# Loading K and V of single-query attention a whole head at a time in the middle of the run, halves elsewhere

## The chip, the cores and the metric

The kernel runs on one core of one Trainium2 chip. The metric is the device time of one execution in microseconds (us). All executions quoted here are of the fast state that runs of one kernel share. "TensorE" is PE, "VectorE" is DVE, "ScalarE" is ACT, "GpSimd" is POOL, and "SyncE" is SP; SP does nothing here but issue loads. The 16 DMA engines are the units that move the data from memory into the core. The "granted clock" is the share of its full speed that TensorE was allowed to run at. A semaphore is a counter on which one engine waits until another, or a load, has raised it.

## The reference

It is attention for a single query position: 16 heads, 8192 keys, head size 256, all bfloat16.

```python
B, H, Sq, Sk, D = 1, 16, 1, 8192, 256      # q, k, v = normal * 0.05
scale = q.shape[-1] ** -0.5
scores = jnp.einsum("bhqd,bhkd->bhqk", q, k) * scale
p = softmax(scores, axis=-1)
return jnp.einsum("bhqk,bhkd->bhqd", p, v)
```

K and V are 4.19 MB each for every head and 134.22 MB in all, and every byte is used once. The arithmetic is small; the reading is the work.

## The kernel before

Each of the 128 partitions holds 64 consecutive keys of a head ("columns" 0 to 63), which are 32 KB of consecutive memory. A head's K or V is loaded as two halves of 32 columns, so a load is 128 rows of 16 KB. There are four places for K halves and four for V halves. DVE computes 24 of the 32 score columns of a half (one multiply-and-sum instruction each), PE the other 8 by transposing them. Two heads later PE multiplies the exponentials with V, one matmul per column (line L612 in the profile of before, L617 after).

The Python below first collects the program of every engine with names of results and of what to wait for; the waits become semaphore waits. SP issues the loads in the order of `items`; a load waits until the half whose place it takes has been used (`kfree`, `ktfree`, `vfree`).

```python
HALF = 32
PE_COLS = 8
GROUP = 4
UNROLL = 2
K_SLOTS = 2 * UNROLL
V_SLOTS = 2 * UNROLL
KT_SLOTS = 4
PROD = 16
FIRST_CUT = (32,)
LAST_CUT = (8, 8, 8, 4, 4)
BEFORE_CUT = (16, 16)
LAG = 4
# ... cut ...
        Kb = [sb([P, HALF * D], dt, "Kb") for _ in range(K_SLOTS)]
        Vb = [sb([P, HALF * D], dt, "Vb") for _ in range(V_SLOTS)]
        # ... cut ...
        def cols(t, h, c0, c1):
            return t[0, h].rearrange("(p j) d -> p (j d)", p=P)[:, c0 * D : c1 * D]
        # ... cut ...
        kseq = [(h, x) for h in range(H) for x in range(2)]
        NIT = 2 * H
        items, nv = [], 0
        for n, kx in enumerate(kseq):
            items.append(("k", *kx))
            while nv <= n - LAG:
                items.append(("v", *kseq[nv]))
                nv += 1
        items += [("v", *kx) for kx in kseq[nv:]]
        n_of = {kx: n for n, kx in enumerate(kseq)}


        def cuts(kind, n):
            if kind == "k" and n == 0:
                return FIRST_CUT
            if kind == "v" and n == NIT - 1:
                return LAST_CUT
            if kind == "v" and n in (NIT - 3, NIT - 2):
                return BEFORE_CUT
            return (HALF,)
        # ... cut ...
        for kind, h, x in items:
            n = n_of[(h, x)]
            slots, sem_l, t, buf = (K_SLOTS, s_k, k, Kb) if kind == "k" else (V_SLOTS, s_v, v, Vb)
            slot = n % slots
            waits = []
            if n >= slots:
                waits = [f"{kind}free{n - slots}"] + ([f"ktfree{n - slots}"] if kind == "k" else [])
            cs = cuts(kind, n)
            at = 0
            for i, wd in enumerate(cs):
                if kind == "k":
                    s = sem_l[slot] if i == 0 else s_first[i - 1]
                else:
                    s = sem_l[slot] if i == len(cs) - 1 else s_last[i + (len(LAST_CUT) - 2 + NIT - 1 - n if n < NIT - 1 else 0)]
                used[id(s)] = used.get(id(s), 0) + 16
                plan.op(
                    "sp",
                    lambda e, b=buf[slot], t=t, h=h, c=x * HALF, at=at, wd=wd: e.dma_start(
                        b[:, at * D : (at + wd) * D], cols(t, h, c + at, c + at + wd)
                    ),
                    f"{kind}{n}.{i}",
                    waits,
                    dma=(s, used[id(s)]),
                )
                at += wd
        # ... cut ...
        # DVE, for each half n and each of its first 24 columns c (the last 8 go to PE):
                    lambda e, slot=slot, c=c, col=col, h=h, r=(ttr - 1) % PROD: e.tensor_tensor_reduce(
                        out=prod[:, r * D : (r + 1) * D],
                        in0=Kb[slot][:, c * D : (c + 1) * D],
                        in1=qbc[:, sl(h) * D : (sl(h) + 1) * D],
                        scale=1.0,
                        scalar=0.0,
                        op0=ALU.mult,
                        op1=ALU.add,
                        accum_out=S[:, col : col + 1],
                    ),
        # ... cut ...
        def pv(n, c0=0, c1=HALF):
            h, x = kseq[n]
            slot = n % V_SLOTS
            a = acc[sl(h)]
            first_free = f"fin{prev(h)}" if prev(h) is not None else None
            for c in range(c0, c1):
                col = sl(h) * J + x * HALF + c
                pe(
                    lambda e, c=c, col=col: e.matmul(
                        a[0:1, 0:D],
                        lhsT=E[:, col : col + 1],
                        rhs=Vb[slot][:, c * D : (c + 1) * D],
                        start=(x == 0 and c == 0),
                        stop=(x == 1 and c == HALF - 1),
                    ),
                    f"vfree{n}" if c == HALF - 1 else None,
                    [f"e{h}", first_free] + landed("v", n, c, c + 1),
                )
        # ... cut ...
        for h in range(H):
            if h >= 2 and h % UNROLL == 0:
                plan.mark("pe")
            if h:
                softmax(h - 1)
            k_turn(2 * h)
            if h:
                softmax2(h - 1)
            k_score(2 * h)
            if h:
                lmm(h - 1)
                if h + 1 < H:
                    q_row(h + 1)
                if h >= 2:
                    pv(2 * (h - 2))
            else:
                lmm(-1, "g-1")
                for a in range(2, H // 2, 2):
                    q_rows([a, a + 1])
            k_turn(2 * h + 1)
            k_score(2 * h + 1)
            if h >= 2:
                pv(2 * (h - 2) + 1)
                final(h - 2)
        # ... cut ...
        n = 2 * (H - 2)
        pv(n)
        softmax(H - 1)
        pv(n + 1, 0, HALF // 2)
        softmax2(H - 1)
        pv(n + 1, HALF // 2, HALF)
        # ... cut ...
        n += 2
        final(H - 2)
        # ... cut ...
        pv(n)
        pv(n + 1)
        final(H - 1)
```

## Time and profile before

| | before |
|---|---|
| time, median of the first 3 runs | 322.27 us (322.23 to 323.55) |
| span in the profile, first to last instruction | 320.8 us |
| bytes loaded | 134.22 MB |
| share of the 16 DMA engines' time in the load queue | 98.7% |
| DVE busy, PE busy | 275.7 us (86%), 221.7 us (69%) |

The DMA part of the profile page of before. The first row is the mean busy share of the 16 DMA engines in tenths, in 40 equal slices of 8 us; the second is what they moved. Then come the packets, and the load queue: packets, MB, share of 16 engines' span.

```profile
DMA  7999999999999999999999999999999999999995
GB/s 304 433 435 420 427 423 431 429 425 429 430 427 429 427 425 427 429 429 427 433 429 429 429 425 425 431 427 429 428 433 427 429 426 425 429 429 429 418 417 200
DMA packets 10126, 134.36 MB, mean 419 GB/s; under 512 B 1138, under 2 KB 1155, under 8 KB 1796
q1 hardware_dynamic: 10080, 134.22, 98.7%
```

The windows view of before. The columns are: stretch, its length, busy time of each engine with the number of instructions, granted share of the TensorE clock, DMA busy share, GB/s.

```profile
40.00:80.00 40.00, 28.75 (x286) 20.38 (x286) 38.65 (x224) 11.95 (x23) 0.00 (x0) 0.96 1.00 426
120.00:260.00 140.00, 101.35 (x1003) 70.86 (x1001) 127.96 (x739) 40.98 (x81) 0.00 (x0) 0.86 1.01 428
304.00:308.00 4.00, 4.00 (x39) 3.09 (x37) 0.28 (x1) 0.34 (x1) 0.00 (x0) 1.00 1.00 418
```

The reading: by the packet records of the trace at least 16 packets, one for each engine, were under way at every moment between 5 and 300 us. With a DMA share of 1.00 at a constant rate, a faster PE or DVE should shorten nothing there; only a change of the loads themselves can. (Run 1 below shows it for PE from the other side: PE was busy for 228.0 us instead of 221.7, and the time stayed.)

The end of the chain of waits of before, in order of time (start us, length us, what):

```profile
263.39 35.08 DMA Vb<-in_v_dram
298.52 5.33 PE acc L612 x32
304.24 0.43 SPq L326
304.72 12.42 DMA Vb<-in_v_dram
317.19 1.92 PE acc L612 x16
319.13 0.47 DVE o L627
```

This piece of the chain looks like PE setting the pace: PE frees a V place at 303.9 us, SP issues the five pieces of the last V half, and the third of them lands 12.4 us after its issue. But the whole half, 2 MB, takes only 4.9 us at 428 GB/s; for the rest of the 12.4 us the load stood in the queue behind others. An earlier issue would only have lengthened its wait in the queue.

### The profile page before, as it was taken

The page shows a single profiled execution, that of the slowest core. Times are in us where ns is not written, and L with a number is a line of the kernel's source. Part 1 is how long each engine was busy: PE and PEld are TensorE (multiplying, and loading weights), DVE is VectorE, ACT ScalarE, POOL GpSimd, SP SyncE. Part 2 cuts the span into 40 slices and gives each one's busy share as a digit, 9 for nine tenths or more (in the row PEclk, how much of TensorE's full clock was granted, in tenths as well). Part 3 has the DMA queues.
Part 4 walks back from the last instruction along what each step waited for, and adds up shares of the span by engine and source line. Part 5 has one row for each costly group of instructions (what it writes and reads, how often), then busy time and mean ns, then how long its engine had stood idle before and what let it go on. Part 6 is the DMA issues. An engine that isn't in the chain of part 4 may idle for free.

```text
span 320.8 us, 6419 instructions
## 1 busy us (share of the span) xinstructions
PE 221.7 (69%) x2166; PEld 155.1 (48%) x2166; DVE 275.7 (86%) x1587; ACT 93.6 (29%) x184; POOL 1.9 (1%) x12
## 2 busy tenths in 40 slices
PE   1745239697686858585977658686667966858897
PEld 0514126565454636463655535464444644535574
DVE  0899999999999999999988988889988889888700
ACT  3453222414233242422142242312423223232010
POOL 2000000000000000000000000000000000000000
PEclk9999999979797989989597987977897797897799
DMA  7999999999999999999999999999999999999995
GB/s 304 433 435 420 427 423 431 429 425 429 430 427 429 427 425 427 429 429 427 433 429 429 429 425 425 431 427 429 428 433 427 429 426 425 429 429 429 418 417 200
DMA packets 10126, 134.36 MB, mean 419 GB/s; under 512 B 1138, under 2 KB 1155, under 8 KB 1796
## 3 DMA queue, kind: packets, MB, share of 16 engines
q1 hardware_dynamic: 10080, 134.22, 98.7%
q8 instruction: 5, 0.08, 0.1%
q14 instruction: 5, 0.04, 0.0%
q10 hardware_dynamic: 36, 0.02, 0.0%
HBM read 134.23 MB, written 0.01 MB: 418 GB/s over the span
## 4 chain that ended last, share of the span: by engine, by line
DVE 49%; DMA 45%; PE 2%; issue 2%; SPq 0%; DVEq 0%
DVE prod L367 46%; DMA Kb<-in_k_dram 30%; DMA Vb<-in_v_dram 15%; PE acc L612 2%; DVE S L367 2%; DVE g L339 0%; SPq L326 0%; DVE recip L348 0%; DVE m L386 0%; DVEq L158 0%; DVE o L627 0%; DVEq L155 0%; DVEq L152 0%
## 5 line engine op out<-in xcount | busy, mean ns | idle before, releaser
L367 DVE CUSTOM_DVE_ANT_0 prod<-Kb,qbc 128x256 bf16<-128x256 bf16 x768 | 269.1, 411 | 27.1 <-DMA Kb<-in_k_dram 24.7
L612 PE MATMUL acc<-Vb,E 128*1 128x256 bf16 x1024 | 146.9, 313 | 7.8 <-DMA Vb<-in_v_dram 7.7
L612 PEld LDWEIGHTS acc<-Vb,E 128*1 128x1 bf16 x1024 | 95.9, 96 | 51.1 <-DMA Vb<-in_v_dram 9.0
L507 ACT ACTIVATE KT<-tp 128x1024 bf16<-128x1024 bf16 x64 | 62.0, 1021 | 116.1 <-PE tp L498 116.1
L367 DVE DVE_READ_ACCUMULATOR2_ANT S<- 128x1 f32 x768 | 56.8, 74 | 0.0
L498 PE MATMUL tp<-identb,Kb 128*128 128x128 bf16 x512 | 38.2, 234 | 5.0 <-DMA Kb<-in_k_dram 5.0
L498 PEld LDWEIGHTS tp<-identb,Kb 128*128 128x128 bf16 x512 | 32.3, 105 | 13.0 <-issue 10.6
L524 PE MATMUL spe<-qcur,KT 128*128 128x1 bf16 x512 | 20.6, 165 | 19.6 <-ACT KT L507 19.6
L563 PE MATMUL misc<-g,ones_row 1*128 1x1 f32 x32 | 7.1, 287 | 37.2 <-DVE g L339 37.2
L524 PEld LDWEIGHTS spe<-qcur,KT 128*128 128x128 bf16 x512 | 16.4, 98 | 24.5 <-ACT KT L507 24.3
L563 PEld LDWEIGHTS misc<-g,ones_row 1*128 1x128 f32 x32 | 5.7, 221 | 40.2 <-DVE g L339 40.0
L635 ACT ACTIVATE o<-acc,recip 1x256 bf16<-1x256 f32 x15 | 7.0, 466 | 60.7 <-PE acc L612 60.7
L552 PE MATMUL misc<-ident,m 128*1 128x128 f32 x34 | 7.1, 293 | 18.2 <-DVE m L386 18.2
L552 PEld LDWEIGHTS misc<-ident,m 128*1 128x1 f32 x34 | 1.8, 81 | 22.0 <-DVE m L386 21.6
L570 ACT ACTIVATE negb<-misc 128x1 f32<-128x1 f32 x16 | 2.7, 171 | 27.6 <-PE misc L563 27.6
L339 DVE TENSOR_REDUCE g<-misc 1x1 f32<-1x128 f32 x17 | 4.7, 274 | 5.2 <-PE misc L552 5.2
L627 DVE TENSOR_SCALAR o<-acc,recip 1x256 bf16<-1x256 f32 x1 | 0.5, 471 | 7.5 <-PE acc L612 7.5
L592 PE MATMUL misc<-ones_col,lsum 128*1 128x1 f32 x34 | 3.2, 164 | 4.1 <-ACT E L577 3.7
L577 ACT ACTIVATE E<-S,negb 128x64 bf16<-128x64 f32 x16 | 5.6, 349 | 0.7 <-ACT negb L570 0.2
L348 DVE RECIPROCAL recip<-misc 1x1 f32<-1x1 f32 x17 | 2.6, 151 | 3.7 <-PE misc L592 3.7
L446 ACT ACTIVATE qbc<-qb 128x256 bf16<-128x256 bf16 x14 | 5.6, 400 | 0.0
L537 ACT ACTIVATE S<-spe 128x16 f32<-128x16 f32 x16 | 3.0, 185 | 7.2 <-PE spe L524 7.2
(26 smaller groups left out, 26.0 us busy)
## 6 DMA issues: line engine op xcount, KB each, us to landing
Kb<-in_k_dram SPq DMA_DIRECT2D x32, 2048.0 KB, 24.3
Vb<-in_v_dram SPq DMA_DIRECT2D x29, 2048.0 KB, 30.5
Vb<-in_v_dram SPq DMA_DIRECT2D x4, 1024.0 KB, 21.1
Vb<-in_v_dram SPq DMA_DIRECT2D x3, 512.0 KB, 11.6
Vb<-in_v_dram SPq DMA_DIRECT2D x2, 256.0 KB, 12.7
q<-in_q_dram ACTq DMA_DIRECT2D x1, 8.0 KB, 3.8
out_dram<-o ACTq DMA_DIRECT2D x1, 7.5 KB
out_dram<-o ACTq DMA_DIRECT2D x1, 0.5 KB
```

Source lines behind the costliest of these rows:

```text
L339: lambda e: e.tensor_reduce(g[0:1, s : s + 1], misc[s][0:1, MT0 : MT0 + P], AX.X, ALU.max),
L367: lambda e, slot=slot, c=c, col=col, h=h, r=(ttr - 1) % PROD: e.tensor_tensor_reduce(out=prod[:, r * D : (r + 1) * D], in0=Kb[slot][:, c * ...
L446: lambda e: e.activation(out=qbc[:, s * D : (s + 1) * D], in_=qb[:, (h - 2) * D : (h - 1) * D], func=ACT.Copy),
L498: lambda e, c=c, hf=hf, i=(b * NH + hf) * P, view=view: e.transpose(view[:, i : i + P], Kb[slot][:, c * D + hf * P : c * D + (hf + 1) * P] ...
L507: lambda e, gn=gn, view=view: e.activation(out=KT[gn % KT_SLOTS][:, :], in_=view[:, 0 : GROUP * D], func=ACT.Copy),
L524: lambda e, b=b, hf=hf, oc=oc, gn=gn: e.matmul(spe[sl(h)][:, oc : oc + 1], lhsT=KT[gn % KT_SLOTS][:, (b * NH + hf) * P : (b * NH + hf + 1) ...
L552: lambda e: e.matmul(misc[s][0:1, MT0 : MT0 + P], lhsT=m[:, s : s + 1], rhs=ident[:, :], start=True, stop=True),
L563: lambda e: e.matmul(misc[s][:, BC0 : BC0 + 1], lhsT=ones_row[0:1, :], rhs=g[0:1, s : s + 1], start=True, stop=True),
L577: lambda e: e.activation(out=E[:, s * J : (s + 1) * J], in_=S[:, s * J : (s + 1) * J], func=ACT.Exp, bias=negb[:, h : h + 1], scale=SCALE, ...
L592: lambda e: e.matmul(misc[sl(h)][0:1, L0 : L0 + 1], lhsT=lsum[:, sl(h) : sl(h) + 1], rhs=ones_col[:, 0:1], start=True, stop=True,),
L612: lambda e, c=c, col=col: e.matmul(a[0:1, 0:D], lhsT=E[:, col : col + 1], rhs=Vb[slot][:, c * D : (c + 1) * D], start=(x == 0 and c == 0), ...
L635: lambda e: e.activation(out=o[0:1, h * D : (h + 1) * D], in_=acc[s][0:1, 0:D], func=ACT.Copy, scale=recip[0:1, s : s + 1],),
```

## The change

The intent: a load packet (what one DMA engine moves in one piece) is as long as a row, as the packet lengths of the traces show below. With rows of 32 KB, half as many packets carry the same bytes. K of heads 7 to 13 and V of heads 5 to 11 are loaded whole, which is 14 of the 32 head tensors. The two halves of a place stay separate for waiting. Where a head comes whole, an empty instruction on POOL waits for it and raises the second half's semaphore too, so that the loops of PE and DVE need not know.

Three things move with it. The loads of a head now stand together (K of a head, then V of an earlier one) instead of half by half, V of head 0 is issued before K of head 2, and V of head 13 after all of K of head 15. PE multiplies both halves of V in one go. And V of heads 14 and 15 comes in 12 pieces instead of 10 (before: 32, 16, 16 and 16, 16, 8, 8, 8, 4, 4 columns).

The core of the diff. Left out are the hunks in which the semaphores are declared and those in which a buffer address is only written in another way.

```diff
--- before
+++ after
@@ -20,10 +20,10 @@
 V_SLOTS = 2 * UNROLL
 KT_SLOTS = 4
 PROD = 16
-FIRST_CUT = (32,)
-LAST_CUT = (8, 8, 8, 4, 4)
-BEFORE_CUT = (16, 16)
-LAG = 4
+WHOLE_K = range(7, 14)
+WHOLE_V = range(5, 12)
+V_CUTS = {14: (16, 16, 16, 16), 15: (16, 8, 8, 8, 8, 8, 4, 4)}
+LAG_FROM = 3
 HEAD_SLOT = {"pe": 0, "dve": 128}
 
 
@@ -190,8 +190,8 @@
         def sem(name):
             return ctx.enter_context(nc.semaphore(name))
 
-        Kb = [sb([P, HALF * D], dt, "Kb") for _ in range(K_SLOTS)]
-        Vb = [sb([P, HALF * D], dt, "Vb") for _ in range(V_SLOTS)]
+        Kb = [sb([P, J * D], dt, "Kb") for _ in range(2)]
+        Vb = [sb([P, J * D], dt, "Vb") for _ in range(2)]
         KT = [sb([P, GROUP * D], BF16, "KT") for _ in range(KT_SLOTS)]
         qb = sb([P, (H - 2) * D], BF16, "qb")
         q16 = sb([H, D], dt, "q16")
# ... cut ...
@@ -249,36 +248,36 @@
         def cols(t, h, c0, c1):
             return t[0, h].rearrange("(p j) d -> p (j d)", p=P)[:, c0 * D : c1 * D]
 
+        def half(t, n, a, b):
+
+            at = n % 2 * HALF * D
+            return t[n // 2 % 2][:, at + a : at + b]
+
 
         kseq = [(h, x) for h in range(H) for x in range(2)]
-        NIT = 2 * H
+
+        def cuts(kind, h):
+            if kind == "v" and h in V_CUTS:
+                return V_CUTS[h]
+            return (J,) if h in (WHOLE_K if kind == "k" else WHOLE_V) else (HALF, HALF)
+
         items, nv = [], 0
-        for n, kx in enumerate(kseq):
-            items.append(("k", *kx))
-            while nv <= n - LAG:
-                items.append(("v", *kseq[nv]))
+        for h in range(H):
+            items.append(("k", h))
+            while nv <= h - (1 if h < LAG_FROM else 2):
+                items.append(("v", nv))
                 nv += 1
-        items += [("v", *kx) for kx in kseq[nv:]]
-        n_of = {kx: n for n, kx in enumerate(kseq)}
-
-        def cuts(kind, n):
-            if kind == "k" and n == 0:
-                return FIRST_CUT
-            if kind == "v" and n == NIT - 1:
-                return LAST_CUT
-            if kind == "v" and n in (NIT - 3, NIT - 2):
-                return BEFORE_CUT
-            return (HALF,)
+        items += [("v", x) for x in range(nv, H)]
 
         def landed(kind, n, c0, c1):
 
+            h, x = kseq[n]
+            if len(cuts(kind, h)) <= 2:
+                return [f"{kind}{h}.{x}"]
             names, at = [], 0
-            if kind == "k" and n and n % K_SLOTS == 0:
-                names = [f"k{n}.0"] + [x for x in landed(kind, 0, c0, c1) if x != "k0.0"]
-                return names
-            for i, w in enumerate(cuts(kind, n)):
-                if at < c1 and at + w > c0:
-                    names.append(f"{kind}{n}.{i}")
+            for i, w in enumerate(cuts(kind, h)):
+                if at < x * HALF + c1 and at + w > x * HALF + c0:
+                    names.append(f"{kind}{h}.{i}")
                 at += w
             return names
 
@@ -306,31 +305,40 @@
 
 
         plan.op("act", lambda e: e.dma_start(q16[:, :], q[0, :, 0, :]), "q", dma=(s_q, 16))
-        for kind, h, x in items:
-            n = n_of[(h, x)]
-            slots, sem_l, t, buf = (K_SLOTS, s_k, k, Kb) if kind == "k" else (V_SLOTS, s_v, v, Vb)
-            slot = n % slots
-            waits = []
-            if n >= slots:
-                waits = [f"{kind}free{n - slots}"] + ([f"ktfree{n - slots}"] if kind == "k" else [])
-            cs = cuts(kind, n)
+        def count(s):
+            used[id(s)] = used.get(id(s), 0) + 16
+            return s, used[id(s)]
+
+        for kind, h in items:
+            sem_l, t, buf = (s_k, k, Kb) if kind == "k" else (s_v, v, Vb)
+            cs = cuts(kind, h)
             at = 0
             for i, wd in enumerate(cs):
-                if kind == "k":
-                    s = sem_l[slot] if i == 0 else s_first[i - 1]
-                else:
-                    s = sem_l[slot] if i == len(cs) - 1 else s_last[i + (len(LAST_CUT) - 2 + NIT - 1 - n if n < NIT - 1 else 0)]
-                used[id(s)] = used.get(id(s), 0) + 16
+                s = sem_l[2 * (h % 2) + i] if len(cs) <= 2 else sem(f"s_{kind}{h}_{i}")
+                waits = []
+                if h >= 2:
+                    for x in range(at // HALF, (at + wd - 1) // HALF + 1):
+                        n = 2 * (h - 2) + x
+                        waits += [f"{kind}free{n}"] + ([f"ktfree{n}"] if kind == "k" else [])
                 plan.op(
                     "sp",
-                    lambda e, b=buf[slot], t=t, h=h, c=x * HALF, at=at, wd=wd: e.dma_start(
-                        b[:, at * D : (at + wd) * D], cols(t, h, c + at, c + at + wd)
+                    lambda e, b=buf[h % 2], t=t, h=h, at=at, wd=wd: e.dma_start(
+                        b[:, at * D : (at + wd) * D], cols(t, h, at, at + wd)
                     ),
-                    f"{kind}{n}.{i}",
+                    f"{kind}{h}.{i}",
                     waits,
-                    dma=(s, used[id(s)]),
+                    dma=count(s),
                 )
                 at += wd
+            if len(cs) == 1:
+
+                plan.op(
+                    "pool",
+                    lambda e: e.nop(),
+                    f"{kind}{h}.1",
+                    [f"{kind}{h}.0"],
+                    dma=count(sem_l[2 * (h % 2) + 1]),
+                )
 
 
         def xmax(h):
# ... cut ...
@@ -603,7 +609,6 @@
 
         def pv(n, c0=0, c1=HALF):
             h, x = kseq[n]
-            slot = n % V_SLOTS
             a = acc[sl(h)]
             first_free = f"fin{prev(h)}" if prev(h) is not None else None
             for c in range(c0, c1):
@@ -612,7 +617,7 @@
                     lambda e, c=c, col=col: e.matmul(
                         a[0:1, 0:D],
                         lhsT=E[:, col : col + 1],
-                        rhs=Vb[slot][:, c * D : (c + 1) * D],
+                        rhs=half(Vb, n, c * D, (c + 1) * D),
                         start=(x == 0 and c == 0),
                         stop=(x == 1 and c == HALF - 1),
                     ),
@@ -660,8 +665,6 @@
                 lmm(h - 1)
                 if h + 1 < H:
                     q_row(h + 1)
-                if h >= 2:
-                    pv(2 * (h - 2))
             else:
                 lmm(-1, "g-1")
                 for a in range(2, H // 2, 2):
@@ -669,6 +672,7 @@
             k_turn(2 * h + 1)
             k_score(2 * h + 1)
             if h >= 2:
+                pv(2 * (h - 2))
                 pv(2 * (h - 2) + 1)
                 final(h - 2)
             elif h == 0:
```

More of the change, by code (lines that the diff above doesn't have):

```diff
@@ L225, in bass_standalone__mha_softmax__decode_kernel @@
         s_v = [sem(f"s_v{i}") for i in range(V_SLOTS)]
-        s_first = [sem(f"s_f{i}") for i in range(len(FIRST_CUT) - 1)]
-        s_last = [sem(f"s_l{i}") for i in range(len(LAST_CUT) + 2 * (len(BEFORE_CUT) - 1) - 1)]
+        s_piece = {}
         s_q = sem("s_q")
@@ L356, in bass_standalone__mha_softmax__decode_kernel @@
         for n, (h, x) in enumerate(kseq):
-            slot = n % K_SLOTS
             if x == 0 and h % UNROLL == 0:
@@ L366, in bass_standalone__mha_softmax__decode_kernel @@
                 dve(
-                    lambda e, slot=slot, c=c, col=col, h=h, r=(ttr - 1) % PROD: e.tensor_tensor_reduce(
+                    lambda e, n=n, c=c, col=col, h=h, r=(ttr - 1) % PROD: e.tensor_tensor_reduce(
                         out=prod[:, r * D : (r + 1) * D],
-                        in0=Kb[slot][:, c * D : (c + 1) * D],
+                        in0=half(Kb, n, c * D, (c + 1) * D),
                         in1=qbc[:, sl(h) * D : (sl(h) + 1) * D],
@@ L485, in k_turn @@
             h, x = kseq[n]
-            slot = n % K_SLOTS
             for gi in range(NG):
@@ L499, in k_turn @@
                                 view[:, i : i + P],
-                                Kb[slot][:, c * D + hf * P : c * D + (hf + 1) * P],
+                                half(Kb, n, c * D + hf * P, c * D + (hf + 1) * P),
                                 identb[:, :],
```

## The prediction

> **What bounds the kernel now.** The loads. The windows view has the 16 DMA engines at a busy share of 1.00 to 1.01 in every 40 us stretch from 40 to 280 us, at 426 to 429 GB/s; the queue table gives the loads 98.7% of the span. K and V are 134.22 MB: at 428 GB/s 313.6 us of the 320.8 us span. The rest is the fill (98 GB/s from 0 to 2 us), a slightly slower end (391 to 426 GB/s from 304 to 316 us, where rows are cut to 8, 4 and 2 KB) and 3.6 us from the last landing (317.2 us) through 16 matmuls, the last scaling and the output. The share of DVE in the chain of waits (49%) misleads: DVE only decides when K places come free, and the queue never ran dry over it. The last V half is issued 12.4 us before it lands (timeline), though 2 MB take 4.9 us.
>
> **What the change does.** 14 of the 32 head tensors (58.7 MB) come in rows of 32 KB instead of 16 KB. The trace's packet records (a load packet is as long as a row) have medians of 84, 161, 313 and 614 ns for 2, 4, 8 and 16 KB. From 8 to 16 KB that is 27.2 bytes/ns per engine, 435 GB/s for 16: the fabric ceiling that the Trainium skill states ("DMA: Bandwidth & Descriptors", Specifications). What remains is 9 to 12 ns per packet whatever its length. The rate agrees: 428 GB/s is 612.5 ns per 16 KB and engine, 10 ns over the 602.4 ns at 435; about 1 ns of it is the 9 ns semaphore packet per transfer.
>
> My estimate: one 32 KB packet in place of two saves 9 ns. A head tensor is 8 such packets per engine, and one semaphore packet fewer: 8 x 9 + 9 = 81 ns. Times 14: 1.13 us. The rate in the whole-head stretches should rise to 431 to 432 GB/s.
>
> Against it: the first halves of V of heads 14 and 15 are cut finer: by the rates of the end, 0.15 us lost. The reordering (V0 before K2, whole heads in turn, V13 after all of K15, the two V halves' matmuls together) moves no bytes and costs nothing, if the queue stays fed. My reckoning: DMA needs 19.6 us per head, DVE 17.2 to 17.8 us, so a whole-head K load is issued with about 10 us of queued work still ahead; V0 needs no free place and adds 10 us of work to the fill; the tightest are the second half of K4 and K7, 4 to 5 us ahead. DVE and PE only wait more. The end behind the last landing is unchanged.
>
> All of the saving is on the critical path, because the DMA engines are: net -1.0 us.
>
> **Prediction: 321.3 us, 80% range 320.3 to 322.5.** Faster by over 2%: 0.01; within 2%: 0.97; slower by over 2%: 0.02.
>
> **What would show it.** Right: packets of 32 KB of about 1,216 ns; 431 to 432 GB/s between roughly 130 and 270 us, 428 elsewhere; DMA share 1.00 throughout; last landing about 1 us earlier, the same 3.6 us after it; DVE idling more before K. Wrong: 32 KB rows recorded as two packets of 614 ns, or stretches with DMA share under 0.98 (starved queue).
>
> **What would make it wrong.** Rows over some length being split; a late release by DVE or PE (K4, K7, or V15 after the late V13 matmuls) that empties the queue; a PE backlog at the end under the throttled clock (0.72 in 300 to 304 us), up to a microsecond; 32 KB packets costing more than the straight line says.

## The result, and the profile after

| | before | after |
|---|---|---|
| time, median of 6 runs | 322.44 us (322.23 to 323.55) | 321.40 us (321.32 to 321.65) |
| ratio, 95% interval | | 0.9965 (0.9951 to 0.9979) |
| again, other rounds | 322.50 us (9 runs) | 321.42 us (5 runs), ratio 0.9965 |
| span in the profile | 320.8 us | 319.9 us |
| packets of the load queue | 10080 | 8352 |
| granted TensorE clock, mean | 0.899 | 0.829 |

A ratio is the mean time of one kernel's fast runs over that of the other's of the same rounds, so it is not quite the ratio of the medians quoted.

The DMA part of the page of after:

```profile
DMA  7999999999999999999999999999999999999995
GB/s 301 434 436 429 422 426 426 424 426 428 427 426 428 434 445 430 438 414 447 414 451 434 418 447 410 451 434 422 438 414 447 414 429 432 428 426 417 422 412 198
DMA packets 8398, 134.36 MB, mean 420 GB/s; under 512 B 946, under 2 KB 963, under 8 KB 1860
q1 hardware_dynamic: 8352, 134.22, 98.6%
```

The queue is as full as before. The GB/s row now swings between 410 and 451, because packets of 1.2 us fall into one slice or the next as a whole: when each packet's bytes are spread over its own time, as below, the rate is even.

The windows view of after, and the end of its chain of waits:

```profile
40.00:80.00 40.00, 29.69 (x286) 21.73 (x286) 38.64 (x224) 11.98 (x23) 0.00 (x0) 0.91 1.00 426
120.00:260.00 140.00, 100.82 (x969) 73.05 (x968) 125.08 (x724) 40.87 (x81) 0.00 (x0) 0.76 1.00 430
304.00:308.00 4.00, 4.00 (x37) 2.98 (x35) 0.28 (x1) 0.00 (x0) 0.00 (x0) 1.00 1.02 419
```

```profile
266.01 26.51 DMA Vb<-in_v_dram
292.65 9.57 PE acc L617 x64
302.61 0.44 SPq L325
303.09 13.14 DMA Vb<-in_v_dram
316.27 1.92 PE acc L617 x16
318.22 0.47 DVE o L632
```

The same end, 0.9 us earlier (316.27 against 317.19).

Two readings go a step below the views, to the packet records of the trace. First, the median length of a load packet:

```text
row, bytes     before ns    after ns
 2048             84           84
 4096            161          161
 8192            313          313
16384            614          613
32768              -         1218
```

Second, how far the loads of a kernel are ahead of those of before at a given moment: the difference of bytes moved by then (each packet's bytes spread evenly over its time), divided by 428 GB/s.

```text
ahead of before, us, at:    60    120    150    190    230    260    290    310    314 us
after                     0.02   0.02   0.25   0.56   0.87   1.11   1.11   0.93   0.85
```

The lead is zero until the first whole head is moved near 120 us, grows steadily to 1.11 us while whole heads are moved, stands still where halves come back, and gives 0.26 us back in the last 25 us. In the stretch from 130 to 250 us the rate by this count is 431.8 GB/s, and 428.3 in before. That is the whole result, seen in one line.

### The profile page after: what moved, and what is told of

Same layout as the page of the kernel before. It is cut to its first block, busy times and chain, and to the rows that moved or that the text cites. A ratio compares the mean times of both kernels' runs of the same rounds, so it can differ in the third digit from the quotient of the medians.

```text
span 319.9 us, 6414 instructions
## 1 busy us (share of the span) xinstructions
PE 227.3 (71%) x2166; PEld 164.0 (51%) x2166; DVE 275.1 (86%) x1587; ACT 93.5 (29%) x184; POOL 1.9 (1%) x12
## 3 DMA queue, kind: packets, MB, share of 16 engines
q1 hardware_dynamic: 8352, 134.22, 98.6%
## 4 chain that ended last, share of the span: by engine, by line
DVE 52%; DMA 41%; PE 4%; issue 2%; SPq 0%; DVEq 0%
DVE prod L374 49%; DMA Kb<-in_k_dram 29%; DMA Vb<-in_v_dram 12%; PE acc L617 4%; DVE S L374 2%; DVE g L347 1%; SPq L325 0%; DVE recip L356 0%; DVE o L632 0%; DVE m L393 0%; DVEq L158 0%; DVEq L155 0%; DVEq L152 0%
## 5 line engine op out<-in xcount | busy, mean ns | idle before, releaser
L617 PE MATMUL acc<-Vb,E 128*1 128x256 bf16 x1024 | 142.9, 310 | 10.3 <-DMA Vb<-in_v_dram 10.1
L374 DVE DVE_READ_ACCUMULATOR2_ANT S<- 128x1 f32 x768 | 55.9, 73 | 0.0
L504 PE MATMUL tp<-identb,Kb 128*128 128x128 bf16 x512 | 46.4, 262 | 4.8 <-DMA Kb<-in_k_dram 4.7
L504 PEld LDWEIGHTS tp<-identb,Kb 128*128 128x128 bf16 x512 | 39.5, 120 | 10.3 <-issue 7.4
L530 PEld LDWEIGHTS spe<-qcur,KT 128*128 128x128 bf16 x512 | 17.2, 103 | 21.1 <-ACT KT L513 20.9
```

Source lines behind the costliest of these rows:

```text
L374: lambda e, n=n, c=c, col=col, h=h, r=(ttr - 1) % PROD: e.tensor_tensor_reduce(out=prod[:, r * D : (r + 1) * D], in0=half(Kb, n, c * D, (c ...
L504: lambda e, c=c, hf=hf, i=(b * NH + hf) * P, view=view: e.transpose(view[:, i : i + P], half(Kb, n, c * D + hf * P, c * D + (hf + 1) * P), ...
L530: lambda e, b=b, hf=hf, oc=oc, gn=gn: e.matmul(spe[sl(h)][:, oc : oc + 1], lhsT=KT[gn % KT_SLOTS][:, (b * NH + hf) * P : (b * NH + hf + 1) ...
L617: lambda e, c=c, col=col: e.matmul(a[0:1, 0:D], lhsT=E[:, col : col + 1], rhs=half(Vb, n, c * D, (c + 1) * D), start=(x == 0 and c == 0), ...
```

## The experiments

Three theories were put against each other. **A** (the prediction's): only the number of packets counts, each costing some 9 ns whatever its length. **B**: the new order pays (V0 early, loads of one head together, V matmuls together), and the row length is an accident. **C**: fewer and larger transfers pay, with fewer issues and waits on SP, and the row length inside them does not matter.

All runs gave the right output. Every run had 5 rounds; the record holds 4 times for run 3 and 6 for run 4. Runs 1 to 4 were on one chip, runs 5 to 8 on another, each with before in the same rounds.

### 1. The order without the long rows

```diff
-WHOLE_K = range(7, 14)
-WHOLE_V = range(5, 12)
+WHOLE_K = ()
+WHOLE_V = ()
```

> The change without its long rows: no head is loaded whole; the new order of the loads, the new order of PE's V matmuls and the finer cuts of V14 and V15 stay. Theory A (only the row length pays; order costs nothing, finer cuts cost 0.15 to 0.25 us): 322.5 us, ratio to the kernel before 1.0005; no lead in bytes over the kernel before up to 290 us, about 0.2 us behind at the end. Rival B (the gain comes from the new order: V0 loaded early, fewer changes between K and V, later V matmuls): about 321.4 us, ratio 0.997.

Measured: 322.49 us (322.42 to 322.68), before 322.37 us, ratio 1.0005 (0.9992 to 1.0018). The loads are 0.07 us behind before at 290 us and 0.21 us behind at 314 us. B falls: without long rows the gain is gone, and the new order by itself neither earns nor costs anything that can be seen. The finer cuts cost 0.14 us of loading at the end by this count.

The same stretch of the windows view of this run:

```profile
120.00:260.00 140.00, 103.65 (x993) 74.76 (x992) 128.92 (x747) 40.66 (x81) 0.00 (x0) 0.76 1.01 428
```

The rate is that of before (428), and the granted clock is that of after (0.76 against 0.86). So it is the new order (of the loads and of PE's V matmuls, which were not separated) that lowers PE's clock, and it costs no time.

### 2. Whole-head transfers made of 16 KB rows

A gap of 256 bytes in the middle of each buffer breaks every row of a whole-head load in two. Transfers, waits, semaphores and order are those of the change. The diff is shortened, and its comments are added here.

```diff
+GAP_EVERY = 32            # columns
+PAD = 128                 # elements, 256 bytes
-        Kb = [sb([P, J * D], dt, "Kb") for _ in range(2)]      # Vb likewise
+        ROW = J * D + J // GAP_EVERY * PAD
+        Kb = [sb([P, ROW], dt, "Kb") for _ in range(2)]
+        def pos(c):
+            return c * D + c // GAP_EVERY * PAD
+        # loads: [p, g, GAP_EVERY * D] on both sides, g = columns // GAP_EVERY;
+        # every reader of column c starts at pos(c)
```

> The change with a gap of 256 bytes in the middle of each K and V buffer, so that a whole-head load is still one transfer of 4 MB with one wait and one semaphore, but consists of 16 KB rows. Theory A: only 14 semaphore packets of 9 ns are saved, so 322.3 to 322.5 us, ratio 1.000; data packets of 16 KB and 614 ns, none of 32 KB, rate 428.4 to 428.6 GB/s throughout. Rival C (fewer, larger transfers and fewer waits and issues pay, not longer rows): 321.4 us, ratio 0.997.

Measured: 322.47 us (322.43 to 322.61), ratio 1.0004 (0.9991 to 1.0017); no packet of 32 KB, those of 16 KB last 615 ns. C falls: the same 14 transfers of 4 MB with 16 KB rows gain nothing that can be seen. The lines of this run, the load queue of its page and its windows view:

```profile
q1 hardware_dynamic: 10144, 134.22, 98.7%
```

```profile
120.00:260.00 140.00, 99.65 (x962) 72.13 (x961) 124.09 (x718) 40.64 (x81) 0.00 (x0) 0.76 1.01 428
```

### 3. The dose turned the other way: 8 KB rows in all heads

```diff
-GAP_EVERY = 32
+GAP_EVERY = 16
```

> As the run with the gap in the middle, but with a gap after every 16 columns, so that every load of 16 columns or more, in all heads, consists of 8 KB rows. The dose made larger the other way: 16 more packets per engine in each of about 30.5 head tensors, at 9.1 ns each, is 4.4 us. Theory A: 326.8 us (ratio 1.0135), 8 KB packets of 313 ns, rate about 422 GB/s throughout. Rivals B and C, to which the row length does not matter: 321.4 to 322.4 us.

Measured: 327.07 us (326.88 to 327.22, 4 fast runs), ratio 1.0144 (1.0129 to 1.0159). The load queue of its page and its windows view:

```profile
q1 hardware_dynamic: 17824, 134.22, 99.2%
```

```profile
120.00:260.00 140.00, 98.43 (x945) 71.42 (x943) 120.53 (x696) 38.94 (x78) 0.00 (x0) 0.76 1.01 422
```

Shorter rows cost what A says. Between this run and the one before there are 7680 packets, 480 for each of the 16 engines, and 4.60 us: 9.6 ns a packet. Between run 2 and the change (321.42 us) there are 1792 packets, 112 for each engine, and 1.05 us: 9.4 ns a packet. This second pair is of different rounds; with each taken against before of its own rounds it is 1.18 us, 10.5 ns, and by the packet records the loads of the change are 1.13 us ahead of those of run 2 at 290 us, 10.1 ns. So the price is known to about 1 ns. That it is about the same in both directions, over a factor of four in row length, is what shows the cause. Where in the path of a packet the price arises, no run shows.

### 4. More whole heads, up to the end

```diff
-WHOLE_K = range(7, 14)
-WHOLE_V = range(5, 12)
+WHOLE_K = (2, 3, 6, 7, 8, 9, 10, 11, 12, 13, 14, 15)
+WHOLE_V = range(0, 13)
```

> The change with whole-head loads wherever I reckon the queue stays fed: K of heads 2, 3 and 6 to 15 (12 instead of 7), V of heads 0 to 12 (13 instead of 7). Theory A: 11 more head tensors at 81 ns each save 0.9 us more: 320.5 us, ratio 0.994, about 431.7 GB/s almost throughout. If the author's limits stood for a real starvation that I overlook, DMA share falls under 0.98 somewhere and the time is 321.4 or more.

Measured: 322.34 us (321.91 to 323.61), ratio 1.0006 (0.999 to 1.0023). A miss by 1.8 us, though not for the reason named in the expectation: the loads are 1.91 us ahead of before at 290 us, near what A has (1.13 + 0.9), and the DMA engines are not idle before 300 us. The end of its chain of waits says where the gain went:

```profile
294.57 0.37 PE spe L530 x8
294.94 13.16 PE acc L617 x96
308.31 1.75 PE acc L617 x16
310.37 1.84 PE acc L617 x16
312.23 7.02 PE acc L617 x64
319.28 0.47 DVE o L632
```

There is no load in it: from 294.9 us to the end PE works off V13, V14 and V15 without once waiting, and is still busy 3 us after the last byte (316.2 us). K15 comes whole, at 286.8 us, where the change has its first half at 282.7 us, 4.0 us earlier, and PE begins V13 at 294.9 instead of 292.7 us and never catches up. In this run the end belongs to PE. Which of K14, K15 and V12 is to blame was not separated.

### 5. The old cuts at the end

```diff
-V_CUTS = {14: (16, 16, 16, 16), 15: (16, 8, 8, 8, 8, 8, 4, 4)}
+V_CUTS = {14: (32, 16, 16), 15: (16, 16, 8, 8, 8, 4, 4)}
```

> The change with the end cut as in the kernel before: V14 in 32, 16, 16 columns and V15 in 16, 16, 8, 8, 8, 4, 4. Theory A: the finer cuts cost 16 more packets per engine and 2 more semaphore packets, 0.15 us, so 321.25 us (321.1 to 321.35 beside 321.4 of the change). If the finer cuts earn something at the end (work for PE earlier), it is 321.4 or more.

Measured: 321.14 us (321.03 to 321.26), before 322.41 us, ratio 0.9961 (0.9948 to 0.9975). That is 0.28 us under the change (321.42 us), in other rounds and on another chip; with each taken against before of its own rounds it is 0.19 us. The finer cuts earn nothing here; they cost.

### 6. More whole heads, but the end left as in the change

```diff
-WHOLE_K = range(7, 14)
-WHOLE_V = range(5, 12)
+WHOLE_K = (2, 3, 6, 7, 8, 9, 10, 11, 12, 13)
+WHOLE_V = range(0, 12)
```

> The run with more whole heads lost its gain at the end: the loads were 1.8 us ahead of the kernel before, but PE did not wait once in its last 64 matmuls. So here K14, K15, V12 are halves again, as in the change, and only the earlier heads are added: K of heads 2, 3 and 6 to 13, V of heads 0 to 11 (22 instead of 14). Theory A with a PE backlog at the end as the cause of that miss: 8 x 81 ns = 0.65 us less than the change, 320.75 us (ratio 0.995), and PE waits for V at the end again. If the loss came from whole loads of the early heads, it stays near 322.3.

Measured: 321.00 us (320.85 to 321.09), ratio 0.9957 (0.9944 to 0.9971). PE waits for V again at the end, as these lines of PE's timeline show (start us, length us, what, idle before it), and 1.3 us of the loss of run 4 is back:

```profile
309.35 4.79 PE L617 MATMUL acc<-Vb,E 128*1 128x256 bf16 x40 [0.64 <-DMA Vb<-in_v_dram]
314.40 1.03 PE L617 MATMUL acc<-Vb,E 128*1 128x256 bf16 x8 [0.26 <-DMA Vb<-in_v_dram]
315.65 1.91 PE L617 MATMUL acc<-Vb,E 128*1 128x256 bf16 x16 [0.22 <-DMA Vb<-in_v_dram]
```

So the miss there came from the late heads, not from the early ones. The size is half a hit: 0.4 us under the change instead of 0.65. Its loads are 1.72 us ahead at 290 us, 0.61 us more than the change's.

### 7. K4 and K5 whole as well

```diff
-WHOLE_K = (2, 3, 6, 7, 8, 9, 10, 11, 12, 13)
+WHOLE_K = range(2, 14)
```

> As the run with more early whole heads, with K4 and K5 whole too. Loads of K4 then wait until DVE has ended all of K2, about 61 us, while the work queued before ends at about 59 us. [...] a gap of 3 to 4 us in the loads: DMA share clearly under 1 near 60 us, all later loads that much later, about 324.0 us (323 to 324.5). If the row length alone counted, it would be 320.6 us.

Measured: 322.22 us (322.0 to 323.15), ratio 1.0004 (0.999 to 1.0017). The direction is right and the size is not: 1.2 us over run 6 instead of 3.3. The windows view of this run around the gap:

```profile
59.00:60.00 1.00, 1.00 (x11) 0.77 (x10) 1.00 (x7) 0.00 (x0) 0.00 (x0) 1.00 1.07 459
60.00:61.00 1.00, 1.00 (x12) 0.76 (x9) 0.97 (x7) 0.00 (x0) 0.00 (x0) 1.00 0.30 115
61.00:62.00 1.00, 0.64 (x5) 0.09 (x2) 0.20 (x1) 0.46 (x1) 0.00 (x0) 1.00 0.87 262
62.00:63.00 1.00, 0.00 (x0) 0.00 (x0) 0.00 (x0) 0.00 (x0) 0.00 (x0) 1.00 1.16 360
```

and SP's timeline there (start us, length us, what):

```profile
60.98 0.33 SPq L325 DMA_DIRECT2D Kb<-in_k_dram  x1
```

DVE ends K2 at 60.95 us, SP issues K4 at 60.98 us, and by the packet records 12 of the 16 engines ran dry by 61.04 us and began K4 from 61.94 us on. The first packets after the restart lasted 1.3 to 2.5 us instead of 1.22. Two of my numbers were off: the work queued before ended at about 61 us and not 59, and the first bytes, for which I had allowed 2 us without having measured it (that clause is cut from the text above), came 0.96 us after the issue began. The Trainium skill ("DMA: Bandwidth & Descriptors", Latency and other measured facts) has about 600 ns to the first byte for loads issued this way; this gap shows 0.63 us from the end of the issuing instruction (60.98 + 0.33 us) and 0.96 us from its start, so the two agree if the page counts from the end. So there is a reason for keeping K4 in halves: its place comes free just too late for a whole load. K5, issued 1.7 us before the queue would have run dry, caused no gap here.

### 8. Both improvements together, and all three side by side

Run 8 has the heads of run 6 and the cuts of run 5.

> The more early whole heads together with the end cuts of the kernel before, the best that theory A can name: 320.6 us, ratio 0.9943. If PE's backlog at the end is the next limit, no better than the run with more early whole heads alone (320.75).

Measured: 320.76 us (320.66 to 320.93), ratio 0.9951 (0.9937 to 0.9965).

The differences between these versions are a few tenths of a microsecond, so the change, run 8 and run 6 were run again unaltered on one chip in the same rounds.

> The change itself once more, unaltered, so that the next two runs are compared with it on one chip in the same rounds; its first runs were not in the rounds of the experiments. Expected: 321.4 us, ratio 0.9965 to 0.997.

> More early whole heads with the old end cuts, unaltered, beside the change on one chip. Theory A: 0.65 us from 8 more whole heads and 0.15 to 0.25 us from the end cuts, 0.8 to 0.9 us under the change: about 320.55 us. As first measured: 320.76 us, 0.65 us under.

> More early whole heads with the new end cuts, unaltered, beside the change on one chip. Theory A: 0.65 us under the change, 320.75 us; as first measured 321.0 us, only 0.4 us under.

| run | time, 5 runs | ratio to before | packets per engine |
|---|---|---|---|
| the change | 321.42 us (321.39 to 321.49) | 0.9965 | 522 |
| more early whole heads, new cuts | 321.07 us (320.89 to 321.11) | 0.9953 | 450 |
| more early whole heads, old cuts | 320.70 us (320.63 to 320.97) | 0.9946 | 432 |

The last one beats both kernels of this study: 0.72 us under the change and 1.8 us under before (322.50 us). At the price of 9.5 ns a packet, 90 packets fewer should give 0.86 us; 0.72 were found. For the 72 packets of the middle row it should be 0.68 us, and 0.35 were found; its loads lead the change's by 0.48 us at 290 us in this pair of profiles. Part of what is missing can be seen at K6. Whole, it is issued at 98.28 us, 1.4 us before the first DMA engine is through with the work queued ahead of it, where the tightest load of the change (the second half of K4) has 5.1 us. The first packets of K6 last up to 2.0 us, and the lead over the change falls there from 0.42 to 0.25 us (0.42 to 0.31 in the last row, 0.49 to 0.43 in run 6). So K6 in halves would be the next thing to try; it was not run. The rest was not settled.

## Why the prediction was right, point by point

- **The time.** 321.3 us predicted, 321.40 and 321.42 us measured; -1.0 us predicted, -1.04 and -1.08 measured. That it is so close is partly luck: the 95% interval of the ratio reaches from 0.7 to 1.6 us of gain, the spans of the two profiles differ by 0.9 us, and the loss by the finer cuts may have been put too low (below).
- **What bounds the kernel.** The DMA engines, as read. Runs 1 to 3 show it from the outside: edits that change how the same bytes are cut move the time by what they change in the loads, and in run 1 PE is busy for 6.3 us more without costing any.
- **The price of a packet.** The packet lengths of 8 and 16 KB gave 12 ns, the rate 9; the prediction took 9, and 9.4 to 10.5 and 9.6 ns were found by runs 2 and 3. A packet of 32 KB was put at 1,216 ns (two of 16 KB less 12 ns) and lasts 1,218. No row of 32 KB was split: the trace has all 1792 of them.
- **The gross saving.** 1.13 us predicted, a lead of 1.11 us at 260 us measured. Rate 431 to 432 GB/s predicted, 431.8 measured by packet records.
- **The ceiling.** The straight line from 8 to 16 KB (301 ns for 8192 bytes, 27.2 bytes/ns, 435 GB/s for 16 engines) agrees with the 435 GB/s of the Trainium skill ("DMA: Bandwidth & Descriptors", Specifications). The same page's "Why small descriptors are slow" speaks of a fixed overhead per packet inside the DMA engine; the runs agree that there is a price per packet, and show that it still counts at 16 KB; whether it is that overhead they do not show.
- **The order costs nothing.** Run 1: ratio 1.0005 with the finer cuts in it.
- **The finer cuts.** This term may have been too small. 0.15 us predicted; the loads of run 1 show 0.14 us of it, and 18 packets per engine at 9.5 ns make 0.17 us. The time shows 0.19 us (run 5 against the change, each against its own before), 0.24 us (run 8 against run 6, same rounds) and 0.37 us (321.07 against 320.70 us, same rounds). What is over 0.17 us is open; it is about as much as these pairs differ among themselves.
- **DVE idling more before K.** Wrong. The waits view, before and then after:

```profile
DVE prod L367 <- DMA Kb<-in_k_dram: 24.7, 15, 8.9
```

```profile
DVE prod L374 <- DMA Kb<-in_k_dram: 23.5, 8, 8.8
```

The waits are half as many and longer each, but their sum went down by 1.2 us. A likely reason, by argument and not by a run: DVE's work is the same (275.7 us busy before, 275.1 after) and it keeps to the pace of the loads, so its idle time is what the loads' time leaves over.
- **The end behind the last landing.** The prediction called 317.2 us the last landing and 3.6 us the rest. That is the last landing for which PE *waited*. By the landings in the trace two more pieces came at 317.78 and 318.41 us while PE was busy; after, the three are at 316.23, 316.87 and 317.49 us. The conclusion (this end is unchanged) held: 2.4 us from the true last landing to the end of the span in both.
- **The margins of the queue.** That K4 is the tightest place was right: in the change its second half is issued 5.1 us before the work queued ahead of it ends (4 to 5 predicted), K7 6.9 us, and between 5 and 300 us the engines were never dry. The estimate behind it was crude by up to 2 us.

## What to carry to other kernels

When the DMA engines are busy all the time at a constant rate, look at packet length against packet size before touching anything else: the fixed part of a packet's time, times the packets that each engine is spared, is what longer rows can give, and here it was about 9.5 ns times 108, 1 us of 322. Longer rows are not free in this kernel, since a place must be wholly free before a whole load and wholly landed before its use. They paid where the queue had work to spare, in the early heads too (run 6). They did not where a place came free too late (K4 in run 7, in part K6) or where the last engine's work had to follow the loads closely (the end, run 4).

## What the Trainium skill lacked or had wrong

- "DMA: Bandwidth & Descriptors", Bandwidth: its table, for loads issued by GpSimd, ends at 425 GB/s for a 16 MB transfer and does not vary the row length. Here, with loads issued by SyncE, one core reading alone held 422 GB/s with 8 KB rows, 428.3 with 16 KB and 431.8 with 32 KB, for transfers of 2 and 4 MB; transfers of 4 MB with 16 KB rows stayed at 428.4.
- The same page, Why small descriptors are slow: it gives the overhead of a packet for 256 bytes (27%) and has joining descriptors into packets worth while only there. (The note above its bandwidth table does have about 10.5 ns a packet, but for the 64 packets of a 4 KB transfer.) The fixed price of a packet (9.4 to 10.5 and 9.6 ns in two pairs of runs) is still 1.5% of the time at 16 KB, and halving the number of packets for 44% of the bytes was worth 0.35% of the run.
- The same page: what it says of descriptors suggests, but no section says outright, that a row of 32 KB goes as one packet. It does (1792 packets of 32768 bytes in the trace, as many as 14 x 128 rows).
- The same page, Latency: it has about 600 ns to the first byte and does not say from when. Restarting a dry queue took 0.63 us from the end of the issuing instruction (0.96 us from its start) to the first packets. That these last longer, here 1.3 to 2.5 us instead of 1.22, it does not have.
- "TensorE: Matmul & The Clock Gate", What's actually happening, says that the clock follows how busy PE has been recently. This case fits that and adds a size: the new order, with the 64 V matmuls of a head in one go instead of two and the loads in another order, lowered the mean granted clock from 0.90 to 0.83 with the same work (before against run 1). By the clock records of the traces TensorE ran at half speed for 65 us of before and for 109 us of run 1, though past 45 us PE was never idle for as long as 3 us in either. What would foretell it was not found here.
